# 64 unused bytes in front of the lower halves of g, in a windowed-attention and feed-forward kernel on one Trainium2 core

## The chip, the core and the metric

The kernel runs on one core of a Trainium2 chip. The core has five engines that follow instruction streams of their own and meet through semaphores: TensorE (PE; its weight loads are listed apart as PEld), VectorE (DVE), ScalarE (ACT), GpSimd (POOL) and SyncE (SP, which here issues all the DMAs). SBUF is the on-chip memory of 128 partitions; an address below is a byte offset within a partition, the same in all of them. PSUM takes TensorE's results.

The metric is the device time of one execution in microseconds. Before the change the median of three runs is 608.89 us (608.73 to 609.63). The profiled execution took 609.05 us, of which 607.3 us lie between its first and last instruction.

## What is computed

The reference, cut to what matters: an attention in which each query sees the 31 keys around it and one summary key and value per block of 32 positions, and behind it a feed-forward layer with a squared ReLU.

```python
k_sum = k.reshape(B, H, nb, 32, D).max(axis=3)
v_sum = v.reshape(B, H, nb, 32, D).mean(axis=3)
scores_l = where(|i - j| < 16, scale * q @ k.T, -1e9)
scores_s = scale * q @ k_sum.T + log(32)
a = softmax(concat([scores_l, scores_s]))
x = (a @ concat([v, v_sum])).transpose(0, 2, 1, 3).reshape(3072, 512)

h = x @ w_in                    # 3072 x 512 times 512 x 2048
r = maximum(h, 0)
g = s * (r * r) + b
out = g @ w_out                 # 3072 x 2048 times 2048 x 512
```

Shapes: 4 batches, 8 heads, 768 positions, 64 per head, so 3,072 tokens of 512 values; all float32.

## The kernel before

The 3,072 tokens are cut into 12 chunks of 256. Each chunk goes through the attention (scores, masks, exponentials, turning the probabilities, values) and then through the feed-forward layer, in 16 slices `f` of the 2,048 hidden values. The work of several chunks is interleaved: while TensorE multiplies chunk c, the other engines prepare chunk c + 1. The order is written out by hand for chunks 0 and 1 (the string `FIRST_ORDER`) and follows from step numbers in a table for chunks 2 to 11; the kernel is built with a manual schedule, so the order of the instructions on each engine is the order of these calls.

[...]

- `hidden(c, f)`, line 460: for each slice f, 12 matmuls into one half of a PSUM tile `ph`: three terms times four blocks of 128 of the 512 inputs. The stationary operand (what TensorE loads as weights, 128 x 128) is a block of `w_l` or `w_h`; the moving operand is 256 columns of `xh` or `xl`.
- `activate`, `scaled`, `upper_rows`, `lower_rows`, lines 464 to 493: for two slices at a time, ReLU and square, times s plus b, then `gh` (the upper half of g, 128 x 512) by a copy that rounds, and `gl` (the lower half) by VectorE's subtraction on line 492.
- `project(c, f)`, line 504: for each slice f and each block t of 128 tokens, three matmuls into the PSUM tile `po`. Here the stationary operand is a 128 x 128 block of `gl` or `gh`, and the moving operand is 512 columns of `w_h` or `w_l`. The terms, in order, are (gl, w_h), (gh, w_l), (gh, w_h). `project_last`, line 514, does the same for the last four slices of the last chunk.

From chunk 2 on the table puts four slices of `hidden` together and then four slices of `project`, so TensorE runs groups of 4 x 12 = 48 matmuls of line 460 and groups of 4 x 6 = 24 matmuls of line 504 in turn, four of each per chunk; the scores and values of the next chunks' attention (lines 301 and 417) come between two groups, once per chunk.

Tiles come from pools. A pool gives each name a fixed place with as many buffers as the call says, in the order in which names are first used, and pools follow each other in the order in which they are opened. The pool `p2` holds, in this order, `vsum`, `ksum`, `rs`, `pT`, `pr`, `mn`, `sums`, `xh`, `xl`, `r`, `gh`, `gl`, `vhalf`, `vmean`; the pool `p3` behind it holds `qk` and `vw`. From the sizes the byte offsets follow, and with them their residues modulo 256, which are the same for all buffers of a name where a buffer's size is a multiple of 256:

| tile | first buffer at byte | buffers x bytes | residue modulo 256 |
|---|---|---|---|
| `w_h` (in `slots`) | 4,352 | 8 x 8,192 | 0 |
| `w_l` (in `wring`) | 69,888 | 17 x 4,096 | 0 |
| `xh`, `xl` | 171,456 and 179,648 | 2 x 4,096 each | 192 |
| `gh` | 191,936 | 4 x 2,048 | 192 |
| `gl` | 200,128 | 4 x 2,048 | 192 |
| `vhalf`, `vmean` | 208,320 and 208,832 | 2 x 256 and 1 x 256 | 192 |
| `qk` | 209,088 | 4 x 2,976 | 192, 96, 0, 160 |
| `vw` | 220,992 | 4 x 2,048 | 64 |

Blocks within a tile of w, x or g begin at multiples of 512 bytes, so all stationary blocks and moving rows of lines 460 and 504 begin at the residue of their tile.

Of the kernel before, what the change touches and what calls it, by code (L numbers as in the profile page):

```python
# [11 lines left out]
F32 = mybir.dt.float32  # L12
# [7 lines left out]
P = 128  # L20
# [24 lines left out]
def windowed_attention_then_relu2_ffn(ctx, tc, qk, vwin, kt, vt, kq, vrow, wp, out):  # L45
# [8 lines left out]
    p2 = ctx.enter_context(tc.tile_pool(name="p2", bufs=2))  # L54
# [48 lines left out]
    w_raw, w_f, w_h, w_l, held = {}, {}, {}, {}, {}  # L103
# [384 lines left out]

    def lower_rows(c, q):
        g, gh = gg[c, q]  # L490
        gl = p2.tile([P, 2 * T], F32R, name="gl", bufs=4)
        nc.vector.tensor_tensor(gl, g, gh.bitcast(F32), ALU.subtract)  # L492
        gg[c, q] = gh, gl
# [68 lines left out]
    def of(fn, *more):  # L562
# [9 lines left out]
        "Ai": of(scale_weights, "in"), "Ao": of(scale_weights, "out"), "A": of(scale_weights, "both"),  # L572
        "Bi": of(convert_weights, "in"), "Bo": of(convert_weights, "out"), "D": of(convert_weights, "both"),
        "Y": hidden_part, "H": hidden, "J": activate, "G": scaled, "a": upper_rows, "b": lower_rows,
        "P": project, "O": evict, "h": upper_weights, "l": lower_weights,
    }
# [58 lines left out]
    for i in range(NF, NC * NF):  # L635
        c, f = divmod(i, NF)

        then(i - i % 4, HID, hidden, c, f)
        if f % 2:
            for stage_of in (activate, scaled, upper_rows, lower_rows):  # L640
                then(i, CHAIN, stage_of, c, f // 2)
        if i >= NC * NF - 4:
            if f == NF - 1:
                then((i + 4) | 3, PROJ, project_last)
            continue
        then((i + 4) | 3, PROJ, project, c, f)
        if f == NF - 1:
            for t in range(T // P):
                then((i + 4) | 3, EVICT, evict, c, t)
# [60 lines left out]
```

## Time and profile before

| what | value |
|---|---|
| median of three runs | 608.89 us (608.73 to 609.63) |
| profiled execution, its own time | 609.05 us |
| its span, first to last instruction | 607.3 us |
| busy: TensorE matmuls, weight loads | 598.1 us (98%), 539.7 us (89%) |
| busy: VectorE, ScalarE, GpSimd | 419.5 us (69%), 275.9 us (45%), 138.9 us (23%) |
| granted TensorE clock | 0.999 of full speed |
| DMA queues' share | 31.0% of 16 engines' span |

How to read it: a row of a group names line, engine, operation, tiles written `<-` tiles read, the shape and the count. A matmul's duration runs from its first row to its last result, and the matmuls are pipelined, so durations overlap: 392 ns is what one of line 504 lasts, while the next one starts earlier. The pace is read from starts, or from a group's length in the chain of waits divided by its count. The ends of matmuls are modelled, so durations are compared with each other and not added up. A row of PEld is the load of the stationary operand for a matmul that starts later.

### The profile page before, as it was taken

What the parts mean: (1) busy time and instruction counts of PE and PEld (TensorE: products, weight loads), DVE (VectorE), ACT (ScalarE), POOL (GpSimd) and SP (SyncE); (2) the same over time, 40 slices, a digit from 0 to 9 for tenths busy, and PEclk for the clock granted to TensorE, in tenths of its full rate; (3) what the DMA queues carried; (4) which work ended last, traced back from release to release, by engine and by line L of the source; (5) the groups of instructions that cost most, each with busy time, mean ns of one, the idle gap of its engine ahead of it and who ended that gap; (6) DMA issues with size and microseconds to landing.
All of it is one profiled execution on the core that took longest, in us unless ns stands there. A gap on an engine that the chain in (4) does not pass through costs nothing.

```text
span 607.3 us, 13540 instructions
## 1 busy us (share of the span) xinstructions
PE 598.1 (98%) x5240; PEld 539.7 (89%) x5240; DVE 419.5 (69%) x1128; ACT 275.9 (45%) x712; POOL 138.9 (23%) x275
## 2 busy tenths in 40 slices
PE   7999999999999999999999999999999999999997
PEld 6798898899989998998999899999998998899896
DVE  6999988789589378668758648847858827832212
ACT  5999998261352262263163254235235235223221
POOL 5420012211511411412141411331151151141110
PEclk9999999999999999999999999999999999999999
DMA  8999723025405016103503211600630500200000
GB/s 337 389 386 389 270 84 113 1 72 156 137 3 186 1 46 225 58 20 107 169 20 100 88 45 64 220 18 20 176 101 1 187 9 12 87 2 1 36 2 35
DMA packets 27281, 66.41 MB, mean 109 GB/s; under 512 B 3856, under 2 KB 4368, under 8 KB 27216
## 3 DMA queue, kind: packets, MB, share of 16 engines
q1 hardware_dynamic: 27216, 65.55, 31.0%
q8 instruction: 41, 0.67, 0.5%
q14 instruction: 24, 0.20, 0.1%
HBM read 59.09 MB, written 6.29 MB: 108 GB/s over the span
## 4 chain that ended last, share of the span: by engine, by line
PE 94%; ACT 3%; DMA 1%; DVE 1%; issue 0%; SPq 0%; DVEq 0%
PE ph L460 43%; PE po L504 43%; PE pav L417 4%; PE ps L301 3%; ACT pr L336 1%; DMA wraw<-in_wp_dram 1%; PE po L514 1%; PE pt L379 0%; PE ph L441 0%; ACT wraw L122 0%; ACT wraw L123 0%; SPq L240 0%; ACT pT L221 0%; DVE pr L346 0%; ACT vsum L221 0%
## 5 line engine op out<-in xcount | busy, mean ns | idle before, releaser
L481 POOL TENSOR_SCALAR r<-r,sb_col 128x512 f32<-128x512 f32 x85 | 69.4, 817 | 392.6 <-ACT r L474 259.6
L468 ACT ACTIVATE r<-ph 128x512 f32<-128x512 f32 x93 | 55.4, 596 | 206.8 <-PE ph L460 172.6
L504 PE MATMUL po<-wh,gh 128*128 128x512 f32 x376 | 148.0, 393 | 0.0
L504 PE MATMUL po<-wh,gl 128*128 128x512 f32 x376 | 147.7, 393 | 0.0
L504 PE MATMUL po<-wl,gh 128*128 128x512 f32 x376 | 147.5, 392 | 0.0
L219 DVE CAST gh<-r 128x512 fp32r<-128x512 f32 x88 | 38.1, 433 | 131.7 <-POOL r L481 130.8
L368 DVE STREAM_TRANSPOSE pT<-pr 32x256 f32<-32x256 f32 x288 | 125.4, 436 | 4.1
L460 PE MATMUL ph<-xh,wl 128*128 128x256 f32 x760 | 119.0, 279 | 0.0
L460 PE MATMUL ph<-xl,wh 128*128 128x256 f32 x760 | 117.8, 277 | 0.0
L460 PE MATMUL ph<-xh,wh 128*128 128x256 f32 x760 | 117.6, 277 | 0.0
L460 PEld LDWEIGHTS ph<-xh,wl 128*128 128x128 f32 x760 | 104.8, 188 | 5.2 <-DVE wl L144 0.3
L460 PEld LDWEIGHTS ph<-xl,wh 128*128 128x128 f32 x760 | 101.3, 188 | 0.0
L460 PEld LDWEIGHTS ph<-xh,wh 128*128 128x128 f32 x760 | 100.7, 188 | 0.0
L504 PEld LDWEIGHTS po<-wh,gl 128*128 128x128 f32 x376 | 70.6, 188 | 15.0 <-issue 1.1
L504 PEld LDWEIGHTS po<-wh,gh 128*128 128x128 f32 x376 | 70.7, 188 | 14.4
L504 PEld LDWEIGHTS po<-wl,gh 128*128 128x128 f32 x376 | 70.6, 188 | 13.8
L336 ACT ACTIVATE pr<-pr,mn 128x120 f32<-128x120 f32 x176 | 67.0, 383 | 22.2 <-DVE mn L323 22.0
L492 DVE TENSOR_TENSOR gl<-r,gh 128x512 fp32r<-128x512 f32 x96 | 69.3, 722 | 4.1 <-ACT gh L221 1.3
L474 ACT ACTIVATE r<-r 128x512 f32<-128x512 f32 x92 | 58.2, 632 | 5.7 <-DVE r L470 2.9
L263 POOL COPY vw<-vsum 24x256 f32<-24x256 f32 x88 | 47.2, 574 | 26.5 <-DMA vsum<-vmean 13.2
L346 DVE TENSOR_TENSOR pr<-pr,rs 128x480 f32<-128x480 f32 x48 | 32.9, 685 | 2.4 <-ACT pr L336 0.5
L221 ACT COPY o<-po 128x512 f32<-128x512 f32 (+1 forms) x23 | 13.1, 570 | 46.3 <-PE po L504 36.0
(94 smaller groups left out, 495.3 us busy)
## 6 DMA issues: line engine op xcount, KB each, us to landing
wraw<-in_wp_dram SPq DMA_DIRECT2D x32, 512.0 KB, 8.3
qk<-in_qk_dram SPq DMA_DIRECT2D x44, 369.0 KB, 5.7
vw<-in_vwin_dram SPq DMA_DIRECT2D x48, 256.0 KB, 3.6
out_dram<-o SPq DMA_DIRECT2D x22, 256.0 KB, 2.0
kraw<-in_kt_dram SPq DMA_DIRECT2D x12, 384.0 KB, 5.5
vraw<-in_vt_dram SPq DMA_DIRECT2D x12, 252.0 KB, 3.1
kq<-in_kq_dram SPq DMA_DIRECT2D x4, 512.0 KB
vraw<-in_vt_dram SPq DMA_DIRECT2D x6, 264.0 KB, 3.2
```

The source lines that it names most:

```text
L219: nc.vector.tensor_copy(out_, in_)
L263: nc.gpsimd.tensor_copy(vw_t[c, p][WIN:KR, e], vsum[bi][WIN : WIN + NB, 2 * p + e, :].unsqueeze(1).to_broadcast([NB, NSUB, D]),)
L336: nc.scalar.activation(pr, pr, AF.Exp, bias=mn_of[c, p][:, n : n + 1], scale=-1.0, accum_out=sm_of[c, p][:, n : n + 1])
L346: nc.vector.tensor_tensor(pr, pr, rs.unsqueeze(2).to_broadcast([P, 4, KR]), ALU.mult)
L368: nc.vector.transpose(to[BLOCK * k : BLOCK * (k + 1), :, rows], src)
L417: nc.tensor.matmul(oi, vw[:KR, e, i, :], pi[:KR], start=True, stop=True)
L460: nc.tensor.matmul(ph, w[:, kc * P : (kc + 1) * P], x[:, kc], start=(n == 0), stop=(n == len(terms) - 1))
L468: nc.scalar.activation(r, ph, AF.Relu)
L474: nc.scalar.activation(r, r, AF.Square)
L481: (nc.vector if other else nc.gpsimd).tensor_scalar(g, g, s_col, b_col, ALU.mult, ALU.add)
L492: nc.vector.tensor_tensor(gl, g, gh.bitcast(F32), ALU.subtract)
L504: nc.tensor.matmul(po[c, t], a[:, t * P : (t + 1) * P], w[:, 512:], start=(f == 0 and n == 0), stop=(f == NF - 1 and n == len(terms) - 1),)
```

## The change

In `lower_rows`, on its first call, a tile of 16 floats (64 bytes) per partition named `gap` is taken from the pool `p2`, just before the first `gl` tile. It is never written or read. The pool places it between `gh` and `gl`, so `gl` and all names that come behind it in `p2`, and the whole pool `p3`, lie 64 bytes higher: `gl` begins at 200,192, which is 0 modulo 256; `gh` stays at 192. `vhalf` and `vmean` move to 0, the four `qk` buffers to 0, 160, 64 and 224, `vw` to 128.

```diff
     def lower_rows(c, q):
         g, gh = gg[c, q]
+        if ("gap", 0) not in held:
+            held["gap", 0] = p2.tile([P, 16], F32, name="gap", bufs=1)
         gl = p2.tile([P, 2 * T], F32R, name="gl", bufs=4)
         nc.vector.tensor_tensor(gl, g, gh.bitcast(F32), ALU.subtract)
         gg[c, q] = gh, gl
```

## Prediction

> **What bounds the kernel now.** I read the page's busy shares first, then its chain of waits, then the chain stage by stage in order of time.
>
> ```profile
> span 607.3 us, 13540 instructions
> PE 598.1 (98%) x5240; PEld 539.7 (89%) x5240; DVE 419.5 (69%) x1128; ACT 275.9 (45%) x712; POOL 138.9 (23%) x275
> PE 94%; ACT 3%; DMA 1%; DVE 1%; issue 0%; SPq 0%; DVEq 0%
> PE ph L460 43%; PE po L504 43%; PE pav L417 4%; PE ps L301 3%; ACT pr L336 1%; DMA wraw<-in_wp_dram 1%; PE po L514 1%; PE pt L379 0%; PE ph L441 0%; ACT wraw L122 0%; ACT wraw L123 0%; SPq L240 0%; ACT pT L221 0%; DVE pr L346 0%; ACT vsum L221 0%
> ```
>
> TensorE runs through 98% of the span, and 86% of the chain that sets the end is two kinds of matmul: `ph` (line 460, hidden layer) and `po` (line 504, projection). Nothing off TensorE is late, so an address matters here only through how fast matmuls follow each other. Next, the chain in order of time, for part of chunk 2 and part of chunk 11 (start us, us, what):
>
> ```profile
> 124.63 5.66 PE ph L460 x48
> 130.29 5.51 PE po L504 x24
> 135.80 5.66 PE ph L460 x48
> ...
> 570.84 5.49 PE po L504 x24
> 576.33 5.47 PE ph L460 x48
> 581.80 5.49 PE po L504 x24
> 587.29 5.47 PE ph L460 x48
> 592.76 5.49 PE po L504 x24
> 598.25 5.51 PE po L514 x24
> ```
>
> The two kinds alternate without a hole. A projection matmul (512 columns) takes 5.49 / 24 = 228.8 ns, a hidden one (256 columns) 5.47 / 48 = 114.0 ns late in the kernel, but 5.66 / 48 = 117.9 ns in chunk 2, with the same tiles at the same addresses (the two tiles each of x's halves take turns). So the pace of identical work has at least two settled values, 0.19 us apart per group of 48. That is the most important thing the profile says for a change of addresses alone. Inside a group the settled pace is read from starts:
>
> ```profile
> 183.88 0.39 PE L504 MATMUL po<-wh,gh 128*128 128x512 f32 x1
> 184.11 0.64 PE L460 MATMUL ph<-xh,wl 128*128 128x256 f32 x4
> 184.58 0.62 PE L460 MATMUL ph<-xl,wh 128*128 128x256 f32 x4
> 185.04 0.62 PE L460 MATMUL ph<-xh,wh 128*128 128x256 f32 x4
> ...
> 189.12 0.62 PE L460 MATMUL ph<-xh,wh 128*128 128x256 f32 x4
> ```
>
> From 185.04 to 189.12 lie 36 matmuls: 4.08 / 36 = 113.3 ns each. The first eight behind a projection group take 185.04 - 184.11 = 0.93 us, 116 ns each: each switch from projection to hidden layer costs about 0.02 us before the quick pace is reached. Twice the settled pace is 226.7 ns for 512 columns; the projection is 2.1 ns above that.
>
> [...]
>
> **The change part by part.** One tile of 16 floats per partition is allocated and never written or read: no instruction, wait, DMA or queue position is added or moved. What moves is everything allocated behind it by 64 bytes: `gl` from 192 to 0 modulo 256, `vhalf` and `vmean` from 192 to 0, the four `qk` tiles from 192, 96, 0, 160 to 0, 160, 64, 224, and `vw` from 64 to 128.
>
> *gl as a stationary operand* is the part that can count. `project` uses three terms per block of 128 tokens: (gl, w_h), (gh, w_l), (gh, w_h). The weights of a term are loaded while the term before it streams:
>
> ```profile
> 183.19 0.39 PE L504 MATMUL po<-wh,gh 128*128 128x512 f32 x1
> 183.19 0.19 PEld L504 LDWEIGHTS po<-wh,gl 128*128 128x128 f32 x1
> 183.42 0.39 PE L504 MATMUL po<-wh,gl 128*128 128x512 f32 x1
> 183.43 0.19 PEld L504 LDWEIGHTS po<-wl,gh 128*128 128x128 f32 x1
> ```
>
> So gl's load lies beside a (gh, w_h) matmul whose moving rows start at 0 modulo 256, or, at a group's start, beside a hidden matmul whose moving x starts at 192. There are 384 such loads (12 chunks, 16 f, 2 blocks). What one of them costs now, from the instructions of line 504 in one steady group (duration ns min/median/max):
>
> ```profile
> L504 PEld LDWEIGHTS po<-wh,gl x8: 187/188/188, 178.5 to 183.2; 128*128 128x128 f32 x8
> L504 PE MATMUL po<-wh,gl x8: 388/388/390, 178.6 to 183.4; 128*128 128x512 f32 x8
> L504 PE MATMUL po<-wl,gh x8: 392/392/392, 178.8 to 183.6; 128*128 128x512 f32 x8
> L504 PE MATMUL po<-wh,gh x8: 393/394/394, 179.1 to 183.9; 128*128 128x512 f32 x8
> ```
>
> The matmul beside gl's load is the longest (394 against 388 and 392), although gh and gl have the same residue. So the order 388, 392, 394 cannot come from the residues alone. The new pairing, however, occurs in the trace of before: the last (gh, w_h) of each group runs beside the load of the hidden layer's w_l, which starts at 0, with moving rows at 0. And the reverse, both at 192, occurs at each start of a group. The two single instructions, with a neighbour each:
>
> ```profile
> L504 PE MATMUL po<-wh,gh x1: 393/393/393, 183.9 to 183.9; 128*128 128x512 f32 x1
> ...
> L460 PE MATMUL ph<-xh,wh x3: 276/276/278, 189.2 to 189.5; 128*128 128x256 f32 x3
> ```
>
> With a load at 0 beside moving rows at 0 the matmul takes 393 ns, against 394 with the load at 192: 1 ns less. With a load at 192 beside moving rows at 192 (the one of 278) it takes 2 ns more than beside a load at 0 (276). All the loads themselves last 188 ns at either residue:
>
> ```profile
> L460 PEld LDWEIGHTS ph<-xh,wl x760: 186/188/192, 36.4 to 591.5; 128*128 128x128 f32 x190
> L460 PE MATMUL ph<-xh,wl x760: 276/276/386, 36.5 to 591.6; 128*128 128x256 f32 x190
> ```
>
> So per load I take -1 ns beside a projection matmul (384 less the 12 x 4 group starts, 336 loads: -0.34 us) and -2 ns at the 48 group starts (-0.10 us): -0.4 us. The bounds go wider, because a pace with several settled values can answer more strongly than one sample shows. Below: the matmul beside gl's load becomes like the shortest of its group, 388 in place of 394, -6 ns x 384 = -2.3 us; or all 1,152 projection matmuls fall to the hidden layer's pace, 2.1 ns x 1,152 = -2.4 us. Above: it becomes like the longest of its line outside a stall:
>
> ```profile
> L504 PE MATMUL po<-wh,gh x376: 388/394/398, 42.7 to 597.9; 128*128 128x512 f32 x188
> ```
>
> 398 - 394 = +4 ns x 384 = +1.5 us. I take -0.4 us, since its rows are of the very pairing that the change makes, and the others are of other places.
>
> *gl as VectorE's output* (line 492) and *the tiles behind it* go together. First line 492 and the waits of line 504, then the instructions of lines 301 and 417:
>
> ```profile
> L492 DVE TENSOR_TENSOR gl<-r,gh 128x512 fp32r<-128x512 f32 x96 | 69.3, 722 | 4.1 <-ACT gh L221 1.3
> ...
>   DVE gl L492: 0.2, 1
> ```
>
> ```profile
> L301 PEld LDWEIGHTS ps<-qk x704: 129/133/133, 14.5 to 502.3; 64*64 64x64 f32 x176
> L301 PE MATMUL ps<-qk x704: 262/263/313, 14.5 to 502.4; 64*64 64x120 f32 x176
> L417 PEld LDWEIGHTS pav<-pT,vw x704: 132/138/138, 27.3 to 548.4; 120*64 120x64 f32 x176
> ```
>
> VectorE is done with gl long before TensorE loads it: in the whole execution the load waited 0.2 us for it, once. The four `qk` tiles already lie at four residues, and line 301, which reads them as both operands, shows hardly a spread between minimum and median. Taking 1 ns each way over all 1,408 matmuls of lines 301 and 417 would be 1.4 us; since four residues leave the minimum 1 ns below the median (262, 263) I take 0. The cover of line 492 is the 5.5 us group in front of gl's use; were it gone, 96 instructions with a tenth more each (mean 722 ns) would be 7 us, but nothing brings them within reach of that.
>
> [...]
>
> **The sum.** The profiled execution took 609.05 us: a span of 607.3 and 1.75 around it. 609.05 - 0.4 = 608.65. It lies 0.16 us above the median of the runs shown, 608.89, so on that scale 608.5; I write 608.6.
>
> **The rivals.**
>
> *A, the projection settles at a quicker pace.* For it: identical hidden work runs at 113.3 and 117.9 ns, so settled paces exist side by side; the projection lies 2.1 ns above the hidden pace per 512 columns, and a third of its loads changes residue. Against: in the trace the projection always comes back to 228.8 ns, and the one sample of the new pairing shows 1 ns. Its price: -2.4 us, and up to 36 x 0.03 = 1.1 us more if the slow start of the hidden groups (5.47 against 48 x 113.3 = 5.44 us) goes from chunks 3 to 11 too: 606.6 down to 605.5. If it takes the pace of chunk 2 (below) away as well, 4 x 0.21 = 0.8 us less: 604.7.
>
> *B, the hidden groups of chunks 3 to 11 stay at the pace of 117.9 ns that chunk 2 shows.* Place: the switch from projection to hidden layer. In chunk 2 a pair of groups takes 5.66 + 5.51 = 11.17 us, in chunk 11 5.47 + 5.49 = 10.96: +0.21 us. With 9 chunks of 4 pairs that is up to 36 x 0.21 = 7.6 us: 616.6 us. It decides from the point at which the last projection matmul of a group hands over in another phase than now; gl's loads lie in every third slot ahead of that. For it: chunk 2 keeps this pace over four groups with the same addresses. Against: the load at the switch itself, w_l at 0, stays as it is, and from chunk 3 on every group came back to 113.3 ns.
>
> *C, the load of gl beside w_h is dearer where both start at 0.* +4 ns x 384 = +1.5 us, and the two other terms drawn along to 398 (+10 and +6) +6.1 us more: 610.5 to 616.7 us. For it: both streams then begin at the same residue. Against: the 393 ns row.
>
> [...]
>
> **How the numbers follow.** A measurement of this kernel can tell about 0.2% from no change (its three runs span 0.15%): 607.7 to 610.1 us. The forecast with D has 0.38; A has 0.35, some 0.08 of it below 605; C has 0.14, mostly from 610.5 to 612.5; B has 0.13, as a lock over part of the chunks as well as over all, so from 611 to 616.6. The likeliest one's own range is 608.2 to 610.1 (the sum less another 0.4, and 1.4 us more for the tiles behind gl). As both signs hold most of the chance together, the range reaches from 604.5 (A with all of its parts, 604.7) to 613.0 (C, and B over half of the chunks, +3.8 us). Some 0.05 is left below and 0.12 above. Faster 0.35, same 0.38, slower 0.27.
>
> **What would show it.** Right: projection groups of 5.48 to 5.49 us, hidden groups of 5.47 from chunk 3 on, medians of line 504 near 388, 392, 393, loads of 188 ns. A: projection groups of 5.44 us or less. B: hidden groups of 5.6 us or more behind chunk 2. C: a (gh, w_h) median of 398 and projection groups over 5.52. Wrong altogether: a difference outside lines 460 and 504, in waits of TensorE on gl, or in lines 301 and 417.

## The result and the profile after

The changed kernel takes 615.9 us (median of four runs, 615.48 to 616.95) against 609.26 us for the kernel before (median of four): a ratio of 1.0106, 95% interval 1.0093 to 1.0119. The prediction was 608.6 us with a range up to 613.0, so it was wrong in direction and outside its range. What happened is the rival B, to which it gave a chance of 0.13. One of the ten runs of the first experiment below, at a granted clock of 0.756, took 743.06 us and is left out of its ratio.

The page of the profiled execution after (616.95 us), the lines that answer to those shown of before:

```profile
span 615.2 us, 13540 instructions
PE 604.5 (98%) x5240; PEld 545.2 (89%) x5240; DVE 418.3 (68%) x1128; ACT 276.5 (45%) x712; POOL 135.0 (22%) x275
...
L460 PE MATMUL ph<-xh,wl 128*128 128x256 f32 x760 | 120.7, 281 | 0.0
L460 PE MATMUL ph<-xl,wh 128*128 128x256 f32 x760 | 120.1, 280 | 0.0
L460 PE MATMUL ph<-xh,wh 128*128 128x256 f32 x760 | 120.1, 280 | 0.0
```

The rows of line 460 of before:

```profile
L460 PE MATMUL ph<-xh,wl 128*128 128x256 f32 x760 | 119.0, 279 | 0.0
L460 PE MATMUL ph<-xl,wh 128*128 128x256 f32 x760 | 117.8, 277 | 0.0
L460 PE MATMUL ph<-xh,wh 128*128 128x256 f32 x760 | 117.6, 277 | 0.0
```

The instructions are the same and TensorE is as full as before (98%). The hidden layer's matmuls, whose operands did not move, are busy for 120.7 + 120.1 + 120.1 = 360.9 us in place of 119.0 + 117.8 + 117.6 = 354.4: 6.5 us of the 7.9 us by which the span grew. The chain of waits of after in order of time, chunk 3 and the end (start us, us, what):

```profile
174.53 5.47 PE ph L460 x48
179.99 5.54 PE po L506 x24
185.54 5.65 PE ph L460 x48
191.19 5.49 PE po L506 x24
196.68 5.65 PE ph L460 x48
...
594.96 5.65 PE ph L460 x48
600.62 5.49 PE po L506 x24
606.11 5.51 PE po L516 x24
```

One hidden group of chunk 3 still takes 5.47 us; the next one takes 5.65 and so do those behind it. The projection groups, whose gl moved, keep their 5.49 us, but for the one behind that hidden group of 5.47 (5.54). In the kernel before, chunk 3 begins so:

```profile
173.31 5.47 PE ph L460 x48
```

Its last projection starts at 598.25 us; here the two starts are 174.53 and 606.11. So 1.22 us are lost ahead of chunk 3 and 6.64 us behind it: 35 groups of 48 at 0.18 to 0.19 us.

The 1.22 us ahead of chunk 3 are partly the projection itself: added up from starts, its groups there take 0.53 us more. The cause of the rest stays open; in the chains of two kernels below that both take 609.1 us, the first and the third, chunk 3 starts at 172.50 and at 173.61 us. In the first two chunks the projection's groups are short (6 to 18 matmuls) and many are entered from the hidden layer's pace of 113.3 ns. The matmuls of TensorE at the first such group, after:

```profile
42.28 0.40 PE L506 MATMUL po<-wh,gl 128*128 128x512 f32 x1
42.52 0.40 PE L506 MATMUL po<-wl,gh 128*128 128x512 f32 x1
...
43.70 0.64 PE L460 MATMUL ph<-xh,wl 128*128 128x256 f32 x4
```

and before:

```profile
42.27 0.39 PE L504 MATMUL po<-wh,gl 128*128 128x512 f32 x1
42.50 0.39 PE L504 MATMUL po<-wl,gh 128*128 128x512 f32 x1
...
43.65 0.64 PE L460 MATMUL ph<-xh,wl 128*128 128x256 f32 x4
```

Six matmuls take 1.42 us in place of 1.38. That is the direct price of gl's place. It is paid when a projection group is entered from the 113.3 ns pace; entered from 117.8 ns, the groups of 24 take 5.49 us here and took 5.51 in chunk 2 of the kernel before.

What differs where a projection group hands over to the hidden layer is seen in the duration of its last matmul (instructions of line 506 at the end of the group ahead of the 5.65 us at 185.54):

```profile
L506 PE MATMUL po<-wl,gh x1: 394/394/394, 184.9 to 184.9; 128*128 128x512 f32 x1
...
L506 PE MATMUL po<-wh,gh x1: 389/389/389, 185.1 to 185.1; 128*128 128x512 f32 x1
```

The last matmul lasts 389 ns. Ahead of the 5.47 us at 174.53 it lasts 393, as it does in chunk 3 of the kernel before:

```profile
L506 PE MATMUL po<-wh,gh x1: 393/393/393, 174.1 to 174.1; 128*128 128x512 f32 x1
```

The kernel before has the 389 too, in chunk 2, ahead of a group of 5.66 us, with the same addresses as in its chunk 3:

```profile
L504 PE MATMUL po<-wh,gl x1: 392/392/392, 135.0 to 135.0; 128*128 128x512 f32 x1
L504 PE MATMUL po<-wl,gh x1: 394/394/394, 135.2 to 135.2; 128*128 128x512 f32 x1
...
L504 PE MATMUL po<-wh,gh x1: 389/389/389, 135.4 to 135.4; 128*128 128x512 f32 x1
```

In chunk 3 of that kernel the three terms last 388, 392 and 394; here 392, 394 and 389. So the three lengths are a beat that runs through the group, not a property of the operands, and a group can end on its short or on its long stroke. That gave theory 3: the stroke on which the projection ends decides the pace of the hidden group behind it, and gl's new place matters because it shifts that stroke. In the kernel before, either pace keeps itself up: a projection group entered at 117.8 ns ends on 389 ns (chunk 2), one entered at 113.3 ns on 393 (chunk 3). In the changed kernel only the slow one does: the group at 179.99, entered at 113.3 ns, ends on 389, and so does every group of 24 behind it.

### The profile page after: what moved, and what is told of

Same layout as the page of the kernel before. It is cut to its first block, busy times and chain, and to the rows that moved or that the text cites. A ratio compares the mean times of both kernels' runs of the same rounds, so it can differ in the third digit from the quotient of the medians.

```text
span 615.2 us, 13540 instructions
## 1 busy us (share of the span) xinstructions
PE 604.5 (98%) x5240; PEld 545.2 (89%) x5240; DVE 418.3 (68%) x1128; ACT 276.5 (45%) x712; POOL 135.0 (22%) x275
## 4 chain that ended last, share of the span: by engine, by line
PE 77%; ACT 10%; DVE 6%; DMA 3%; issue 2%; POOL 1%; SPq 0%; POOLq 0%; ACTq 0%; DVEq 0%
PE po L506 35%; PE ph L460 34%; PE pav L417 4%; ACT pr L336 3%; PE ps L301 3%; ACT wraw L122 2%; ACT wraw L123 2%; DMA wraw<-in_wp_dram 2%; DVE pT L368 2%; DVE wf L132 1%; DMA vsum<-vmean 1%; PE po L516 1%; DVE gl L494 1%; DMA kq<-in_kq_dram 1%; DVE vhalf L172 1%
## 5 line engine op out<-in xcount | busy, mean ns | idle before, releaser
L460 PE MATMUL ph<-xh,wl 128*128 128x256 f32 x760 | 120.7, 281 | 0.0
L460 PE MATMUL ph<-xl,wh 128*128 128x256 f32 x760 | 120.1, 280 | 0.0
L460 PE MATMUL ph<-xh,wh 128*128 128x256 f32 x760 | 120.1, 280 | 0.0
L460 PEld LDWEIGHTS ph<-xh,wl 128*128 128x128 f32 x760 | 106.2, 189 | 5.2 <-ACT r L474 0.4
L460 PEld LDWEIGHTS ph<-xh,wh 128*128 128x128 f32 x760 | 103.2, 190 | 0.0
L263 POOL COPY vw<-vsum 24x256 f32<-24x256 f32 x88 | 45.1, 550 | 27.7 <-DMA vsum<-vmean 12.2
```

The lines of the kernel that those rows point to most:

```text
L263: nc.gpsimd.tensor_copy(vw_t[c, p][WIN:KR, e], vsum[bi][WIN : WIN + NB, 2 * p + e, :].unsqueeze(1).to_broadcast([NB, NSUB, D]),)
L460: nc.tensor.matmul(ph, w[:, kc * P : (kc + 1) * P], x[:, kc], start=(n == 0), stop=(n == len(terms) - 1))
```

## The experiments

Theories 1 (the place of gl) and 2 (the place of the tiles behind it) ask whose address does it; 3 asks how it reaches matmuls that did not move. The gap is written as in the change unless a diff shows something else, and the residues given are modulo 256.

**Only the tiles behind gl move.**

```diff
         gl = p2.tile([P, 2 * T], F32R, name="gl", bufs=4)
+        if ("gap", 0) not in held:
+            held["gap", 0] = p2.tile([P, 16], F32, name="gap", bufs=1)
```

> The 64 unused bytes lie behind gl instead of in front of it: gl stays at 192, everything behind it moves as in the change. Theory 1 (gl's place among the operands of lines 460 and 504 decides): as before, 609 us, hidden groups of 5.47 us from chunk 3 on. Theory 2 (any move of the tiles behind gl, qk and vw, disturbs the attention blocks and with them the pace): as after, 615.9 us, hidden groups of 5.65 us.

609.07 us, ratio 0.9997 (0.9982 to 1.0011). Two groups of chunk 3:

```profile
183.46 5.47 PE ph L460 x48
188.93 5.49 PE po L506 x24
```

Theory 2 is out: `vhalf`, `vmean`, `qk` and `vw` may lie 64 bytes further without a price.

**Both halves of g move.**

```diff
     def upper_rows(c, q, other=False):
         g = gg[c, q]
+        if ("gap", 0) not in held:
+            held["gap", 0] = p2.tile([P, 16], F32, name="gap", bufs=1)
         gh = p2.tile([P, 2 * T], F32R, name="gh", bufs=4)
```

> The 64 unused bytes lie in front of gh: gh and gl both at 0 modulo 256, w at 0, x at 192. Theory 1a (what counts is that gl and gh have different residues): as before, 609 us, since they are equal again. Theory 1b (what counts is gl's residue against that of the moving w): as after or slower, 615.9 us or more, since now all three loads of a slice start at w's residue. Theory 2: 615.9 us.

613.91 us, ratio 1.0074 (1.0049 to 1.0100). The chain in order of time:

```profile
183.74 5.65 PE ph L460 x48
189.40 5.44 PE po L506 x24
194.84 5.65 PE ph L460 x48
200.49 5.44 PE po L506 x24
```

The two products go opposite ways. The projection is quicker than in any kernel before it, 5.44 / 24 = 226.7 ns, twice 113.3 to within 0.1 ns; all three terms last 389 ns and the beat is gone. The hidden layer sits at 5.65 us. Theory 1a is out. So is 1b, which expected 615.9 us or more: the equal residue of g and w is good for the projection itself.

**Everything moves by 64.**

```diff
+    const.tile([P, 16], F32, name="gap")
     ident = const.tile([P, P], F32, name="ident")
```

> 64 unused bytes ahead of all tiles: every residue is 64 higher than before (w 64, x, gh and gl 0), all differences are as before. If only differences between the two streams that TensorE reads count: 609 us, hidden groups of 5.47 us. If the residue itself counts: another time, 603 to 617 us; gl at 0 is then no harm by itself only if this is 609.

609.09 us, ratio 0.9994 (0.9973 to 1.0015):

```profile
184.56 5.47 PE ph L461 x48
190.03 5.49 PE po L505 x24
```

gh and gl lie at 0 here as in the kernel of 613.9 us, without harm. So it is the difference between the places of the loaded block and of the moving rows that counts, not the place.

**The changed kernel, with two terms of the last slice exchanged.**

```diff
         terms = [(gl, w_h[f]), (gh, w_l[f]), (gh, w_h[f])]
+        if f % 4 == 3:
+            terms = [terms[1], terms[0], terms[2]]
```

> The changed kernel, but in every fourth slice (the last of a projection group) the three terms come as (gh, w_l), (gl, w_h), (gh, w_h): addresses and amount of work as after, only the place of gl's loads in the last 6 of 24 matmuls differs. Theory 3 (the length of the last projection matmul, that is the phase in which it hands over, decides the pace of the 48 hidden matmuls behind it): where the last one lasts 393 ns or more the hidden group takes 5.47 us, and the kernel about 609 to 611 us; where it lasts 389 it stays at 5.65 us and 615.9. Rival (the addresses of the hidden layer's neighbours set its pace directly, whatever the order): 5.65 us and 615.9 us, with no tie to the last matmul's length.

611.32 us, ratio 1.0039 (1.0022 to 1.0055). The end of a projection group, and the chain:

```profile
L508 PE MATMUL po<-wh,gl x1: 388/388/388, 195.1 to 195.1; 128*128 128x512 f32 x1
...
L508 PE MATMUL po<-wh,gh x1: 395/395/395, 195.3 to 195.3; 128*128 128x512 f32 x1
```

```profile
184.72 5.45 PE ph L460 x48
190.18 5.56 PE po L508 x24
195.73 5.45 PE ph L460 x48
```

The last matmul lasts 395 ns and the hidden groups are back at 5.45 us, with every address as in the changed kernel. The projection pays for it with 5.56 us, mostly since its groups are now entered from the 113.3 ns pace (the one such group of 24 in chunk 3 of the changed kernel took 5.54), so the change is not undone: 4.6 us of the 6.6 are.

**The kernel before, with two matmuls of each projection group placed earlier.** The counterpart: all addresses of before, and only the order touched.

```diff
     def hidden(c, f):
...
+        if f % 4 == 3 and NF * c + f - 7 >= 2 * NF:
+            project(*divmod(NF * c + f - 7, NF), upto=2)
         for n, (w, x, kc) in enumerate(terms):
```

`project` here emits its six matmuls only up to `upto` and later the rest.

> The kernel before with all its addresses; only the order changes: from chunk 2 on, the first two of the 24 matmuls of a projection group come 12 matmuls earlier, ahead of the last hidden slice, so that the group that hands over has 22. Same instructions, same work. Theory 3 (the phase at the handover decides): in a group entered from the pace of 113.3 ns the 22nd matmul is one of the 388 to 389 ns kind, so the hidden groups behind it take 5.65 us, and the kernel 613 to 617 us. Rival (addresses decide, order does not): hidden groups of 5.47 us and 609 to 610 us.

614.10 us, ratio 1.0072 (1.0054 to 1.0090). The chain of chunk 3, and the last matmul of the first group of 22 shown in it:

```profile
190.35 5.03 PE po L509 x22
195.38 4.24 PE ph L462 x36
199.62 0.46 PE po L509 x2
200.08 1.41 PE ph L462 x12
201.50 5.13 PE po L509 x22
206.63 4.10 PE ph L462 x36
```

```profile
L509 PE MATMUL po<-wl,gh x1: 394/394/394, 194.8 to 194.8; 128*128 128x512 f32 x1
...
L509 PE MATMUL po<-wh,gh x1: 389/389/389, 195.0 to 195.0; 128*128 128x512 f32 x1
```

With no address changed, the order alone costs 0.7%. The first group of 22 ends on 389 ns and the 36 hidden matmuls behind it take 4.24 us, 117.8 ns each. Theory 3 had expected that of every group; it happens in every second one. A group of 22 entered from the 117.8 ns pace runs at 5.13 / 22 = 233 ns, another settled value, ends on 392 ns, and the 36 behind it take 4.10 us, 113.9 ns. One thing does not fit: the groups of two that end on 392 ns are followed by 12 matmuls at 117.5 ns (the 1.41 us), so the length of one matmul marks the stroke only behind a longer group.

Counted over the traces of ten kernels whose x and w lie as far apart as before (the two compared kernels, the four runs from the first to the fourth above, and the four with gl at 64, gl at 224, gh at 0 and the split tiles below), for every hidden run of at least 12 matmuls behind a projection matmul: behind 388 or 389 ns, 211 end at the pace of 117.8 ns and 2 at 113.3; behind 392 ns or more, 301 end at 113.3 and 8 at 117.8 (the split is drawn at 116 ns, mean of the last eight). Another 8 stand behind 390 or 391 ns, 7 of them at 113.3. The kernel just above also has x and w so far apart and is not in this count: there 19 runs behind 388 or 389 ns end at 117.8 ns, and behind 392 or more 54 end at 113.3 and 19 at 117.8, all 19 behind a group of two.

**Other places for x and g.** These ask which difference belongs to which pace, and whether one gives 226.7 and 113.3 ns together. x and g at 0, by the gap in front of `xh`:

```diff
         if p == 0:
+            if ("gap", 0) not in held:
+                held["gap", 0] = p2.tile([P, 16], F32, name="gap", bufs=1)
             xt[c] = p2.tile([P, NKC, T], F32R, name="xh", tag="xh")
```

> The 64 unused bytes lie in front of xh: x, gh and gl all at 0 modulo 256, as w is. Theory 4 (where the loaded block and the moving rows start at the same residue the pace settles at one value, 113.3 ns per 256 columns, as the projection did with g at 0): projection groups of 5.44 us and hidden groups of 5.44 to 5.47 us, 605.5 to 607 us. Theory 5 (the equal residue only moves the handover; the hidden layer keeps its two paces and takes the slow one behind a last matmul of 389 ns): projection 5.44, hidden 5.65 us, 614 us.

619.64 us, ratio 1.0177 (1.0159 to 1.0195). Hidden groups:

```profile
185.78 5.75 PE ph L462 x48
191.54 5.47 PE po L506 x24
```

Theory 4 is out, and 5 too: 5.75 / 48 = 119.8 ns is a pace not seen before. With equal residues the projection's 512 moving columns were quicker (5.44 us a group with x at 192, 5.47 here, against 5.49 before) and the hidden layer's 256 slower (5.75 against 5.47). gl alone at 64 (the gap of 32 floats) and at 224 (of 8 floats):

```diff
-            held["gap", 0] = p2.tile([P, 16], F32, name="gap", bufs=1)
+            held["gap", 0] = p2.tile([P, 32], F32, name="gap", bufs=1)   # 8 in the second
```

> 128 unused bytes in front of gl: gl at 64 modulo 256, gh at 192. If only equality with w's residue (0) does the harm: 609 us. If any difference between gl's and gh's residue does it: 613 to 617 us. By the handover law in either case: the last projection matmul lasts 389 ns where the hidden groups take 5.65 us, 392 or more where they take 5.47.

> 32 unused bytes in front of gl: gl at 224 modulo 256, half the step of the change. If the residue counts in steps of 64 bytes: 609 us, as before. If it counts in steps of 32 or less: another time, 606 to 617 us.

613.35 us, ratio 1.0079 (1.0057 to 1.0100), and 617.70 us, ratio 1.0147 (1.0129 to 1.0164). With gl at 64 the hidden groups keep 5.46 us, the last matmul of most projection groups lasts 392 ns, and the projection takes 5.60: the loss is all in the projection. With gl at 224 the projection takes 5.54, the last matmul 389 and the hidden groups 5.65 to 5.66. So 32 bytes already count, and both ways of losing exist. The mirror, gh at 0 and gl at 192:

```diff
     def upper_rows(c, q, other=False):
+        gl = p2.tile([P, 2 * T], F32R, name="gl", bufs=4)
+        if ("gap", 0) not in held:
+            held["gap", 0] = p2.tile([P, 16], F32, name="gap", bufs=1)
         gh = p2.tile([P, 2 * T], F32R, name="gh", bufs=4)
...
```

`lower_rows` then uses this `gl` and allocates none.

> The mirror of the change: gh at 0, gl at 192 (gl is given its place ahead of gh, nothing else differs). Two of the three loads of a slice then start at w's residue, in place of one as in the change. If the loads act one by one in the same direction: projection pace between the change's 229.1 and the 226.9 ns of both at 0. By the handover law: 5.65 us per hidden group and about 614 to 616 us if the last projection matmul lasts 389 ns, 5.47 us and 607 to 609 us if it lasts 392 or more.

612.60 us, ratio 1.0059 (1.0039 to 1.0079). The projection takes 5.54 to 5.55 us, more than with one load or three at w's residue, so the loads don't act one by one. Its beat no longer has a fixed place: of the hidden runs counted, 11 stand behind 389 ns at 117.8 ns, 41 behind 393 or more at 113.3, and one behind 394 at 117.8. Then the tiles of g split by pairs of slices, even ones at 0, odd ones at 192:

```diff
-        gh = p2.tile([P, 2 * T], F32R, name="gh", bufs=4)
+        if ("gap", 0) not in held:
+            for name in ("gh_odd", "gl_odd"):
+                held[name] = p2.tile([P, 2 * T], F32R, name=name, bufs=2)
+            held["gap", 0] = p2.tile([P, 16], F32, name="gap", bufs=1)
+        gh = p2.tile([P, 2 * T], F32R, name="gh_odd" if q % 2 else "gh_even", bufs=2)
```

and `gl` likewise.

> gh and gl of even pairs of slices at 0, of odd pairs at 192 modulo 256, under tile names of their own with two buffers each: in a projection group the first 12 matmuls read stationary tiles at 0, as with both at 0, the last 12 at 192, as before. Theory 3 (the handover decides): the last matmul again lasts 393 ns, the hidden groups take 5.47 us, though half of the g tiles lie as in the kernel that ran at 613.9; with the first half at 226.7 ns a projection group takes 5.46 to 5.48 us and the kernel 607.5 to 609 us. Rival (g tiles at 0 anywhere slow the hidden layer): 5.65 us and 613 us.

616.64 us, ratio 1.0129 (1.0114 to 1.0144). The last matmul, and the chain:

```profile
L508 PE MATMUL po<-wh,gh_odd x1: 389/389/389, 185.4 to 185.4; 128*128 128x512 f32 x1
```

```profile
180.32 5.47 PE po L508 x24
185.79 5.65 PE ph L460 x48
```

The projection is as expected, 5.47 us. The last 12 matmuls read their operands where the kernel before has them, but the last three last 392, 394 and 389 ns, in place of 388, 392 and 393 in its chunk 3: the group ends on the short stroke, and the hidden groups take 5.65. What failed is the guess of the stroke, not its tie to the hidden pace; taken alone, this run does not exclude the rival. Last, x at 224 with g at 0 (8 floats in front of `xh`, 8 in front of `gh`), and x and g at 64 (32 floats in front of `xh`):

> 32 unused bytes in front of xh and 32 in front of gh: x at 224, both halves of g at 0, w at 0. The projection should settle at 226.7 ns as with g at 0. For the hidden layer: if the two paces 113.3 and 117.8 belong to x being 192 away from w, another pace appears (between 113.3 and 120 ns); if they belong to any unequal residue, 117.8 ns behind a last matmul of 389 ns and 613.9 us.

> 128 unused bytes in front of xh: x, gh and gl at 64, w at 0, so the sign of the difference is turned against before. If only the size of the difference counts: 609 us with 113.3 and 228.8 ns. If its direction counts: another pair of paces, 604 to 620 us.

616.59 us, ratio 1.0128 (1.0111 to 1.0145): hidden groups 5.68 us (118.3 ns), projection 5.49, in which the matmuls of (gl, w_h), the first term, last 394 ns on the mean and the two others 391. And 620.91 us, ratio 1.0196 (1.0180 to 1.0211): hidden 5.65, projection 5.60, behind last matmuls of 396 to 399 ns, and one of 392. Here the tie to 392 and more does not hold, so it was seen only with x 192 bytes from w. A difference of 64 one way is not the same as 64 the other way.

| residue of w, x, gh, gl | projection x24, us | hidden x48, us | time, us |
|---|---|---|---|
| before: 0, 192, 192, 192 | 5.49 | 5.47 | 609.3 |
| all 64 higher: 64, 0, 0, 0 | 5.49 | 5.47 | 609.1 |
| the change: 0, 192, 192, 0 | 5.49 | 5.65 | 615.9 |
| 0, 192, 0, 0 | 5.44 | 5.65 | 613.9 |
| 0, 192, 0, 192 | 5.55 | 5.47, some 5.65 | 612.6 |
| 0, 192, 192, 64 | 5.60 | 5.46 | 613.4 |
| 0, 192, 192, 224 | 5.54 | 5.65 | 617.7 |
| 0, 224, 0, 0 | 5.49 | 5.68 | 616.6 |
| 0, 0, 0, 0 | 5.47 | 5.75 | 619.6 |
| 0, 64, 64, 64 | 5.60 | 5.65 | 620.9 |

No placement tried is quicker than the kernel before by more than the noise, and none has the projection's 226.7 ns together with the hidden layer's 113.3.

## Why the prediction was wrong, point by point

- *What bounds the kernel*: right. TensorE's succession of matmuls is all there is, and the observation that identical work has two settled paces (5.66 and 5.47 us) was the key to the result.
- *The price per load*: this is the step that failed. The sum holds gl's 384 loads alone, at -0.4 us, and puts the pace of the hidden groups, whose operands do not move, at nothing. The runs showed 35 hidden groups at 5.65 in place of 5.47 us: 6.6 of the 7.9 us by which the profiled span grew. The price itself was taken from single instructions (393 against 394 ns, 278 against 276). Those lengths stand in the trace, but a matmul's length here is a stroke in a beat that runs through the three terms (388, 392 and 394 ns); one neighbour changed for one matmul says nothing of the beat that follows when it is changed in each slice. The very pairing of the 393 ns lasts 389 ns in chunk 2 of the same trace (at 135.4 us, above). The prediction had noted that 388, 392 and 394 "cannot come from the residues alone" and did not draw that conclusion.
- *Two slips without weight*: the trace of before has 59 projection groups where the sum takes 48, and on the scale of the runs the sum gave 608.5 where 608.6 was written.
- *The bounds*: the pace behind the -2.4 us, a projection at twice the hidden layer's 113.3 ns, does occur, with both halves at 0 (5.44 us a group). In the change itself the projection groups stayed at 5.49 us.
- *Rival B*: right in place (the switch from projection to hidden layer), in its reason (gl's loads shift the phase) and in size: 0.21 us a pair was named, 11.14 - 10.96 = 0.18 us was measured (5.65 + 5.49), over 35 groups. Its mis-set term is the chance. Held against it was that from chunk 3 on every group came back to 113.3 ns; but what kept them there was the stroke on which the projection ends, and that is what the change touches. That its 616.6 us for all chunks lies so near to the 615.9 is partly luck: 1.22 us of the growth lie ahead of chunk 3, where B has nothing. The range's upper end of 613.0 took in only half of it.
- *Rival C*: wrong from chunk 3 on (groups of 5.49 us, in which (gh, w_h) lasts 393 and 389 ns in turn and not 398), right in small for groups entered from 113.3 ns (1.42 against 1.38 us for six).
- *Rival D* (no change, 609.0 us, counted within the forecast's 0.38): no run shows that a move of gl by 64 bytes is without effect. With gl at 0 and at 224 in place of 192 the kernel took 615.9 and 617.7 us. With w and x in place and only g and the tiles behind it moved, a projection group takes from 5.44 to 5.60 us, so the place of the loaded block does matter here.
- *The tiles behind gl, and VectorE*: right. Moved alone they cost nothing (0.9997), and lines 301 and 417 kept their medians (263 and 222 ns).

What stays open is the hardware behind the beat: why a group settles at one value or another, and what makes the relative place count. That the relative place of the two streams and the order set the stroke, and that with x 192 bytes from w the stroke goes with the pace of the next group, is shown, with the groups of two as an exception. Which stroke a new order or placement will end on was not foreseen (the split tiles). That the two reads of SBUF hinder each other is not shown by any run. A matmul's end is modelled in these profiles, so the 389 and 393 ns are marks and not measurements of lost time.

## What to carry to other kernels

Where one engine is full and its profile shows identical groups of work at two settled paces, treat a change of addresses or of order as a possible change of that pace: its price is then the difference of the paces times the groups (here 0.18 to 0.19 us times 35), not a sum over the instructions that moved, and it may fall on instructions that did not, as it did here on the hidden layer's. Look at how a group ends and what the next one does behind each ending, and give the pace that already occurs somewhere in the kernel a large chance. An allocation that adds bytes in front of operands of TensorE should be timed like any other change, and judged by group lengths in the chain of waits.

## What the runs showed that was not expected

In these runs the paces at which the matmuls settled went with the difference between the loaded block's and the moving rows' places: 113.3, 117.8, 118.3 or 119.8 ns at 256 columns, and 226.7, 228.8 or 233 ns at 512; 32 bytes were enough to change it (617.7 us with gl at 224), and shifting both together by 64 did nothing (609.1 us). The residues are given modulo 256 for order's sake: no run shows that a shift of 256 is harmless, and one of 128 is not (x and g at 64 in place of 192: 620.9 us against 609.3). The same addresses ran at either of two paces (113.3 and 117.8; 228.8 and 233) for a whole group, depending on how the group was entered. The equal residue gave the quickest pace seen at 512 moving columns (226.7 ns with x at 192, but 227.9 and 228.8 with x at 0 and 224) and the slowest at 256 (119.8).
